# Five units of 128 channels, two k columns a step, and a token mix with tokens on the partitions

## The chip, the cores and the metric

The kernel runs on one core of a Trainium2 chip. The metric is the device time of one execution in microseconds (us). Medians have their lowest and highest value beside them. The engines are TensorE (PE, its weight loads PEld), VectorE (DVE), ScalarE (ACT), GpSimd (POOL) and SyncE (SP), which issues most DMAs.

## The reference, cut to what matters

```python
# x: 2048 tokens x 640 channels, bf16; F = 1728, Fh = 864
h = layernorm(q) * (1 + ca) + sa                  # sa..gb: six rows of silu(c) @ w_mod
k_shift = short_conv(k, shift_k)                  # four taps
kv = k_shift * v
y  = irfft(rfft(pad(kv)) * rfft(pad(ssm_k)))[:S]  # long convolution over the tokens
y  = y + kv * ssm_D
x  = q + ga * (h * y)
h  = layernorm(x) * (1 + cb) + sb
z  = gelu(h @ w_in)                               # 640 -> 1728
z2 = layernorm(z[..., 864:])
g  = w_sp @ z2 + b_sp                             # token mix: 2048 x 2048
x  = x + gb * ((z[..., :864] * g) @ w_out)
```

I name its parts by time: the **start** (tables, short convolution, first transforms), the **mixer** (the long convolution by matrix products: stage 1, a forward product `pu`, a frequency product `T` on VectorE, an inverse product `pz`), the **hole** (TensorE has little to do while the last unit goes through residual, layer norm and transposes), the **gated part** (the projection to `z`) and the **back end** (token mix and output projection).

## The kernel before

Channels go through the mixer in units of 128, 192, 192 and 128. Every instruction of the front part is put into a plan with a planned cost and a priority; a list scheduler fixes each engine's order at build time.

```python
UNITS = ((0, 128), (128, 192), (320, 192), (512, 128))
SLOTS = dict(X=3, X1=3, KH=17, T=4, Z=2, ZT=2, wm=1, big=2, dg=2, st1=2, s1=2, pu=3, pz=2, py=1)
# ...
# stage 1: two channel groups per PSUM tile, two such tiles, emptied by ScalarE
ps = new(name, "s1", [P, 2, NJ * 8], F32)
for i in range(2):
    mm(ps[:, i, :], tl[X][:, cp + i, :], F1flat, True, True)
# ... e.copy(dst, ps)
# one k column of one unit
pu = new(name, "pu", [P, 2, DUM], F32)
mm(pu[:, :, 0:du], M2[:, 0, kc, :], x[:, 2 * kc:2 * kc + 2, 0:du], True, False)
mm(pu[:, 0, 0:du], M2[:, 2, kc, :], xi, False, False)
mm(pu[:, 1, 0:du], M2[:, 1, kc, :], xr, False, True)
# ... product: T_ = pu x KH, [P, 2, 2, du], on VectorE; then six matmuls of the inverse product
# residual and statistics of a unit: one statistic per unit and token tile
op({"DVE": 120 + 0.85 * du}, lambda e, n=n: e.bn_stats(out=st2[:, n, u, :], in_=xt[:, n, d0:d0 + du]), ...)
# ...
# back end: channels on the output partitions (seven channel tiles, the last one short)
for tci in range(S // TC):
    for ft in range(NFT):
        ps = psB.tile([P, TC], F32, tag="mm", bufs=6, name="ps")
        for st_i in range(NT):
            nc.tensor.matmul(ps[:fsz[ft], :], lhsT=tl["hz%d" % (st_i // TB)][:, zo:zo + fsz[ft]],
                             rhs=wT[:, st_i, tci * TC:(tci + 1) * TC], start=(st_i == 0), stop=(st_i == NT - 1))
        # VectorE: add the bias, multiply by z1T[ft]
for n in range(NT):
    ...  # output projection of token tile n, all 16 after the whole mix
```

## Time and profile before

| kernel before, profiled execution | us from the span's start |
|---|---|
| first inverse product | 39.03 |
| end of the last inverse product | 147.6 |
| first matmul of the gated part | 166.93 |
| first matmul of the token mix | 231.21 |
| span | 362.2 |

The median is 364.14 us (363.43 to 364.27, 3 executions). The page's rows, the table by stage, the three forms and VectorE's hole are shown in the prediction below. A row of slices has one digit for each fortieth of the span, the busy share in tenths. In a list in order of time the first number is the start, the second the length of a run of like instructions, and a bracket at the end says how long the engine idled before them and what it waited for.

What such a list shows as a matmul's length has a modelled end. The true price is read from starts: a group of six forward matmuls starts 0.44 us before what follows it, although its length is given as 0.60. The prices read so in the kernel before (median ns from one matmul's start to the next) are 25 for one column, 29 for 64, 56 for 128, 82 for 192, 109 for 256, 136 for 320, 162 for 384, 183 for 432 and 216 for 512; at them its 2374 matmuls come to 310.9 us. I therefore also sum the streaming price of all matmuls between two instants, as the prediction does, and compare it with the elapsed time.

The mixer's waits of TensorE as the profile lists them, in the kernel before (total, times, longest):

```profile
PE s L269 <- ACT X L430: 1.6, 7, 0.3
PE s L269 <- DMA wm<-in_w_mod_dram: 0.5, 1, 0.5
PE pz L269 <- DVE T L465: 0.3, 2, 0.2
PE py L269 <- DMA ZT<-Z: 0.2, 1, 0.2
```

That is 2.6 us. The mixer streams 100.5 us in 108.5, so 8 us are lost. The list shows less because it counts a wait from the modelled end of the matmul before it, 0.16 us after the next could have started, and leaves out what is then under 0.15 us. For instance, the rows of the list in order of time have four stage-1 fills of 256 columns from 67.67 and the next from 68.72: 1.05 us for 0.44 us of streaming, with one bracket of 0.18. Counted from start to start, the waits over 0.06 us in the kernel before are 30 and cost 7.8 us: 15 of them, 4.6 us, are for ScalarE's stage-1 copies, and eight, 1.4 us, for `T`. Between the others TensorE goes from one tile's matmuls to another's without loss.

### The profile page before, as it was taken

To read this page: it belongs to the slowest core of one execution; us is meant where nothing else is said; L and a number is where in the kernel's file an instruction comes from. 1 tells how busy PE (TensorE), PEld (TensorE's weight loads), DVE (VectorE), ACT (ScalarE), POOL (GpSimd) and SP (SyncE) were. 2 spreads that over 40 slices of the span, in tenths; PEclk is the share of its full clock that TensorE was granted. 3 is DMA by queue.
4 is the path that set the end of the run, shared out by engine and by line. 5 is a ranking of instruction groups with operands and counts; after the bars stand their busy time and mean duration, and the time that the engine had idled before them with its cause. 6 is when DMAs were issued, how large, how long until landed. Compare 5 with 4: busy or idle time off the path is not lost.

```text
span 362.2 us, 6081 instructions
## 1 busy us (share of the span) xinstructions
PE 328.2 (91%) x2374; PEld 201.8 (56%) x2374; DVE 223.0 (62%) x492; ACT 153.3 (42%) x324; POOL 117.1 (32%) x133
## 2 busy tenths in 40 slices
PE   1777999899999999709999999999999999999996
PEld 0225787567778888504545654444444444446774
DVE  6769999673749889999893883024233232334553
ACT  6359878967797865605557555300000000000000
POOL 7773611159208999661131011740000000000000
PEclk9989999999999999966999999999999999999999
DMA  7889959869889379100009999510000000000221
GB/s 123 186 242 235 194 201 225 157 91 251 175 223 212 114 157 179 48 1 2 0 9 224 219 205 243 153 31 0 14 2 0 14 2 0 0 2 36 93 91 72
DMA packets 110084, 40.08 MB, mean 111 GB/s; under 512 B 95368, under 2 KB 109288, under 8 KB 110056
## 3 DMA queue, kind: packets, MB, share of 16 engines
q1 hardware_dynamic: 108560, 39.18, 49.4%
q0 software_dynamic: 192, 0.52, 0.7%
q8 instruction: 18, 0.29, 0.3%
q10 hardware_dynamic: 1304, 0.00, 0.2%
q14 instruction: 10, 0.08, 0.1%
HBM read 16.63 MB, written 5.24 MB: 60 GB/s over the span
## 4 chain that ended last, share of the span: by engine, by line
PE 82%; DVE 7%; ACT 6%; POOL 2%; DMA 1%; issue 1%; POOLq 0%; DVEq 0%; ACTq 0%
PE ps L863 27%; PE pu L269 19%; PE pz L269 16%; PE s L269 9%; PE ps L875 8%; ACT X L430 4%; DVE st L698 1%; PE s L787 1%; DMA ZT<-Z 1%; POOL T L366 1%; PE py L269 1%; DVE gh L652 1%; PE pu L680 1%; POOL T L365 1%; DVE T L465 0%
## 5 line engine op out<-in xcount | busy, mean ns | idle before, releaser
L863 PE MATMUL ps<-wT,X 128*128 128x512 bf16 (+1 forms) x336 | 77.1, 379 | 0.0
L866 DVE TENSOR_TENSOR gt<-ps,bsp 128x512 bf16<-128x512 f32 (+1 forms) x28 | 19.3, 691 | 75.2 <-PE ps L863 54.6
L465 DVE TENSOR_TENSOR T<-pu,KH 128x512 bf16<-128x512 f32 (+1 forms) x64 | 50.7, 819 | 14.9 <-PE pu L269 12.3
L863 PEld LDWEIGHTS <-X 128*128 128x128 bf16 (+1 forms) x336 | 34.1, 101 | 38.4
L269 PE MATMUL pu<-X,M 128*128 128x128 bf16 (+3 forms) x384 | 48.6, 254 | 1.1 <-ACT KH L453 1.1
L430 ACT CAST X<-s 128x512 bf16<-128x512 f32 x80 | 44.0, 592 | 8.0 <-PE s L269 7.2
L269 PE MATMUL pz<-T,G 128*128 128x192 bf16 (+3 forms) x384 | 45.2, 255 | 0.3 <-DVE T L465 0.3
L269 PEld LDWEIGHTS <-X 128*128 128x128 bf16 x280 | 26.4, 100 | 21.8 <-issue 10.4
L269 PEld LDWEIGHTS <-M 128*128 128x128 bf16 x384 | 33.0, 98 | 8.9 <-issue 1.4
L269 PEld LDWEIGHTS <-G 128*128 128x128 bf16 x384 | 32.2, 98 | 6.8 <-DVE T L465 0.8
L269 PE MATMUL s<-F1bd,X 128*128 128x256 bf16 x160 | 29.5, 276 | 5.5 <-DVE big L526 2.3
L482 ACT CAST Z<-pz 128x256 bf16<-128x256 f32 (+1 forms) x64 | 27.2, 430 | 14.2 <-PE pz L269 12.7
L269 PE MATMUL s<-big,dg 128*128 128x512 bf16 x80 | 23.5, 441 | 10.6 <-DMA big<-in_A_k_dram 8.0
L863 PE MATMUL ps<-wT,Z 128*128 128x512 bf16 (+1 forms) x112 | 28.7, 379 | 0.0
L453 ACT CAST KH<-pu 128x256 bf16<-128x256 f32 (+1 forms) x64 | 25.3, 432 | 5.3 <-PE pu L269 4.4
L629 POOL TENSOR_TENSOR gh<-gh,gca_bf 128x512 bf16<-128x512 bf16 (+1 forms) x16 | 22.2, 1400 | 11.2 <-DVE gca_bf L595 11.2
L877 DVE TENSOR_TENSOR ot<-ps,xt 128x320 bf16<-128x320 f32 x32 | 15.7, 491 | 14.2 <-PE ps L875 14.2
L695 POOL TENSOR_TENSOR xt<-xt,gh 128x768 bf16<-128x768 bf16 (+1 forms) x12 | 17.7, 1506 | 20.1 <-DVE gh L656 20.1
L875 PE MATMUL ps<-w_o,G 128*128 128x320 bf16 (+1 forms) x128 | 22.7, 299 | 0.0
L269 PEld LDWEIGHTS <-big 128*128 128x128 bf16 (+1 forms) x140 | 14.1, 102 | 15.2
L629 POOL TENSOR_TENSOR gh<-gh,gsa_bf 128x512 bf16<-128x512 bf16 (+1 forms) x16 | 22.2, 1399 | 0.8
L269 PEld LDWEIGHTS <-dg 128*128 128x128 bf16 x80 | 8.5, 108 | 21.6 <-issue 8.8
(138 smaller groups left out, 447.9 us busy)
## 6 DMA issues: line engine op xcount, KB each, us to landing
wm<-in_w_mod_dram SPq DMA_DIRECT2D x8, 400.0 KB, 3.9
kv_scr<-big SPq DMA_DIRECT2D x5, 512.0 KB, 3.3
xt<-in_A_q_dram SPq DMA_DIRECT2D x2, 1280.0 KB, 6.4
out_dram<-ot SPq DMA_DIRECT2D x16, 160.0 KB, 1.8
big<-in_B_w_in_dram SPq DMA_DIRECT2D x2, 1080.0 KB, 7.0
X<-in_A_ssm_k_dram SPq DMA_DIRECT2D x2, 768.0 KB, 9.6
X<-kv_scr SPq DMA_DIRECT2D x2, 768.0 KB, 6.6
wm<-in_w_mod_dram SPq DMA_DIRECT2D x4, 320.0 KB, 3.3
```

Source lines behind the costliest of these rows:

```text
L269: nc.tensor.matmul(o, lhsT=w, rhs=x, start=start, stop=stop)
L365: e.tensor_scalar(tl[v][:], tl[v][:], pidx[:, 0:1], 1.0 / 8192.0, op0=ALU.mult, op1=ALU.mult)
L430: e.copy(dst, tl[name][:].rearrange("p i (j g) -> p i j g", g=8))
L453: op({"ACT": act_cost(2 * du)}, lambda e: e.copy(tl[KH][:, :, 0:du], tl[pk][:, :, 0:du]), r=[pk], w=[KH], t=t)
L465: e.tensor_tensor(T_[:, :, :, 0:du], tl[pu][:, :, None, 0:du].to_broadcast([P, 2, 2, du]), tl[KH][:, None, :, 0:du].to_broadcast([P, 2, 2, ...
L482: op({"ACT": act_cost(2 * du)}, lambda e: e.copy(tl[Z][:, 0:du // 4, 2 * kc:2 * kc + 2, :], tl[pz][:, :, 0:du] .rearrange("p r (q c) -> p ...
L629: lambda e, vec=vec, o=o: e.tensor_tensor(gvu, gvu, vec[:, None, d0:d0 + du].to_broadcast([P, TB, du]), op=o),
L695: op(eng, lambda e: e.tensor_tensor(sl, sl, gh[:, g * TB:(g + 1) * TB, d0:d0 + du], op=ALU.add), r=[("gh", (u, g))], w=[("xt", (u, n)) for ...
L863: nc.tensor.matmul(ps[:fsz[ft], :], lhsT=tl["hz%d" % (st_i // TB)][:, zo:zo + fsz[ft]], rhs=wT[:, st_i, tci * TC:(tci + 1) * TC], start=(s ...
L866: nc.vector.tensor_tensor(gt[:fsz[ft], :], ps[:fsz[ft], :], bsp_bc[:fsz[ft], :], op=ALU.add)
L875: nc.tensor.matmul(ps[:, :HS], lhsT=z1T[ft][:fsz[ft], n * P:(n + 1) * P], rhs=w_o[:fsz[ft], ft, h * HS:(h + 1) * HS], start=(ft == 0), sto ...
L877: nc.vector.tensor_tensor(ot[:, h * HS:(h + 1) * HS], ps[:, :HS], xt[:, n, h * HS:(h + 1) * HS], op=ALU.add)
```

## The change

The intent is to make the units equal (five of 128 channels), so that a step can take two k columns in one PSUM tile (fewer, wider instructions on VectorE and ScalarE), to give one statistic to two units, and to turn the back end round: tokens on the output partitions leave no short channel tile, the bias becomes a column, product and bias are one VectorE instruction, and each token tile is projected soon after its mix. The product then has channels in the free dimension and must be turned; a DMA transpose does it, and TensorE for the last tile. The first half of the gated projection is turned likewise. The priorities of the plan are new.

```diff
-UNITS = ((0, 128), (128, 192), (320, 192), (512, 128))
+NU = 5
+DU = 128
+KP = 2
+S1C = 4
-SLOTS = dict(X=3, X1=3, KH=17, T=4, Z=2, ZT=2, wm=1, big=2, dg=2, st1=2, s1=2, pu=3, pz=2, py=1)
+SLOTS = dict(X=4, X1=4, KH=9, T=4, Z=3, ZT=1, ZTp=2, wm=1, big=2, dg=2, st1=2, s1=1, sm=2, pu=2, pz=2)
...  (new priorities WANT; SECOND says how much later a second choice of engine may be)
@@ stage 1: four channel groups per PSUM tile, one such tile
-                    ps = new(name, "s1", [P, 2, NJ * 8], F32)
-                    for i in range(2):
+                    ps = new(name, "s1", [P, S1C, NJ * 8], F32)
+                    for i in range(S1C):
                         mm(ps[:, i, :], tl[X][:, cp + i, :], F1flat, True, True)
@@ forward product: two k columns
+                pu = new(name, "pu", [P, KP, 2, DU], F32)
+                for k in range(KP):
+                    kc = st * KP + k
+                    mm(pu[:, k], M2[:, 0, kc, :], x[:, 2 * kc:2 * kc + 2, :], True, False)
+                    mm(pu[:, k, 0], M2[:, 2, kc, :], x[:, 2 * kc + 1, :], False, False)
+                    mm(pu[:, k, 1], M2[:, 1, kc, :], x[:, 2 * kc, :], False, True)
@@ frequency product: one instruction of 1024
+                T_ = new(T, "T", [P, KP, 2, 2, DU])
+                e.tensor_tensor(T_[:], tl[pu][:, :, :, None, :].to_broadcast([P, KP, 2, 2, DU]),
+                                tl[KH][:, :, None, :, :].to_broadcast([P, KP, 2, 2, DU]), op=ALU.mult)
@@ statistics: units 0 and 1 together, 2 and 3 together, 4 alone
+            if u not in (1, 3, 4):
+                return
+            us = range(u - (u < 4), u + 1)
...  (gated part: z1 with tokens on the partitions)
@@ back end
+    def mix(t):
+        u = us[t % UB]
+        for fc in range(NFC):
+            ps = psB.tile([P, 512], F32, tag="mm", bufs=4, name="ps")
+            for s_ in range(NT):
+                nc.tensor.matmul(ps[:, :FC], lhsT=wTs[t][:, s_, :], rhs=tl["z2_%d" % (s_ // TB)][...],
+                                 start=(s_ == 0), stop=(s_ == NT - 1))
+            nc.vector.scalar_tensor_tensor(u[:, sl], ps[:, :FC], bcol[:, t:t + 1], z1[t][:, sl], op0=ALU.add, op1=ALU.mult)
+        if t < NT - 1:
+            nc.sync.dma_start_transpose(uTs[t][:], u[:])
+            return
+        ...  (last tile: seven TensorE transposes and one copy)
+    for t in range(NT + 2):
+        if t < NT:
+            mix(t)
+        if t + WB - 1 < NT:
+            load_w(t + WB - 1)
+        if t >= 2:
+            project(t - 2)
```

## The prediction

> **What bounds the kernel now.** I read the page first, then the groups by form, then a table by stage, then the lists in order of time of TensorE and of VectorE around the two places where TensorE waits.
>
> The page's busy shares and its row of slices:
>
> ```profile
> PE 328.2 (91%) x2374; PEld 201.8 (56%) x2374; DVE 223.0 (62%) x492; ACT 153.3 (42%) x324; POOL 117.1 (32%) x133
> ...
> PE   1777999899999999709999999999999999999996
> DVE  6769999673749889999893883024233232334553
> ```
>
> TensorE (PE) is full from slice 5 to the end (a slice is 9.06 us), except the first 40 us and one hole at slices 17 and 18, around 150 to 165 us, where VectorE (DVE) is at 9. The stages, cut where the lists show the work change:
>
> ```profile
> 8.00:39.00 31.00, 23.54 (x138) 12.16 (x138) 25.61 (x67) 20.98 (x49) 19.53 (x29) 0.94 0.98 212
> 39.00:148.00 109.00, 105.40 (x1110) 82.93 (x1108) 84.66 (x153) 82.03 (x194) 60.90 (x55) 1.00 0.83 182
> 148.00:167.00 19.00, 7.59 (x98) 5.91 (x99) 18.70 (x55) 6.60 (x10) 9.65 (x7) 0.72 0.00 1
> 167.00:231.40 64.40, 64.40 (x363) 33.67 (x361) 42.05 (x109) 37.98 (x66) 11.88 (x16) 0.98 0.72 148
> ```
>
> Columns after the stretch and its length: busy time of PE, PEld, DVE, ACT, POOL (instructions), granted clock, DMA share, GB/s. The sequence mixer (39 to 148 us) is PE's, and so are the gated part (167 to 231) and everything after it. Start and hole belong to chains of other engines. Three forms set what PE's time is worth:
>
> ```profile
> L863 PE MATMUL ps<-wT,X 128*128 128x512 bf16 x288 | 66.1, 379 | 0.0
> L430 ACT CAST X<-s 128x512 bf16<-128x512 f32 x80 | 44.0, 592 | 8.0 <-PE s L269 7.2
> L465 DVE TENSOR_TENSOR T<-pu,KH 128x768 bf16<-128x768 f32 x32 | 29.7, 953 | 12.2 <-PE pu L269 11.0 <-ACT Z L482 0.7 <-PE pz L269 0.4
> L465 DVE TENSOR_TENSOR T<-pu,KH 128x512 bf16<-128x512 f32 x32 | 21.0, 685 | 2.7 <-PE pu L269 1.3 <-ACT KH L453 0.5 <-issue 0.3
> ```
>
> 379 ns is one matmul's modelled duration, not its price: the chain of waits has the token mix as one piece,
>
> ```profile
> 231.38 96.69 PE ps L863 x448
> 328.07 30.57 PE ps L875 x224
> ```
>
> so 512 columns cost 96.69/448 = 215.8 ns and 320 columns 30.57/224 = 136.5 ns.
>
> [...] 215.8 and 136.5 ns, and 182.7 ns for 432 columns (5 in 0.9135 us in the gated part). I price matmuls so. [...] in the hole the granted clock is 0.72 and the first five 432-column matmuls take 1.8 us. [...] The two T rows give (953-685)/256 = 1.05 ns an element, about 149 ns fixed, so 1024 elements should take 1.22 us. [...] The change gives each step more columns but fewer buffers, which is my main doubt.
>
> **The change, part by part.** All numbers of instructions are from the two programs' order lists.
>
> *PE work.* [...] all of before is 310.9 us in 2374 matmuls, of after 307.5 in 2657. So the span of 362 holds 51 us that is not PE streaming, and the change removes only 3.4 us of streaming:
> - Token mix: 448 matmuls of 512 become 512 of 432 (tokens on the output partitions, so no short seventh channel tile): 96.7 to 512 x 182.7 ns = 93.5, -3.2 us.
> - First half of the gated projection, turned likewise: 140 of 512 (30.2 us) to 160 of 432 (29.2), -1.0 us.
> - Units of 128 instead of 192: the same columns, 192 more matmuls in the mixer, +0.5 us; seven small transposes for the last tile, +0.4.
>
> *The back end.* Each of 16 tiles has 5.85 us of mix and 1.91 us of projection, issued two tiles late. Its product goes out by a DMA transpose on the queue that also brings the next weight tile. Before, the 16 weight transposes took SyncE 1.7 to 3.0 us each to issue and landed after 4.3 to 6.2; with the product's smaller one and a store I estimate 5 us of queue per 7.76 us tile, and the result is wanted about 12 us later, so nothing waits. VectorE falls from two instructions (691 and 425 ns) to one of 432 from PSUM (0.60 us by the fit): idle there anyway, worth nothing. The last tile's product must pass VectorE and PE's transposes while PE waits: about 0.9 us of wait, in +1.3 with the transposes. Mix, projection and end: 124.1 + 1.3 + the 3.5 us that before has after its last matmul = 128.9, against 130.8: **-1.9 us**.
>
> *The gated part.* 61.75 us of streaming against 62.8, plus the 1.65 us that before loses to the cold clock: 63.4 against 64.45, **-1.0 us**.
>
> *The mixer.* Per pair of k columns VectorE's product is one instruction of 1024: 40 x 1.22 = 48.9 against 50.7 us. ScalarE's stage-1 copies go from 80 x 592 ns to 40 of 1024 (0.85 ns an element by the KH rows, about 1.03 us): 41 against 47 us. Both lie beside PE. What counts is what PE had done when the first inverse product (pz) started: before 15.6 us of streaming at 39.03, after 20.6, because more taps and forward products stand ahead of it. But VectorE also has five more tap products (5 x 0.62), one more layer norm statistic (1.07), four normalisations (4 x 0.42) and one copy less (0.65) ahead of its first T: 5.2 us, of which I let half go into its idle time there (some 7 us before its first T at 37.86): 39.0 + 2.5 = 41.5 us for the first pz (estimate). From there before ran 100.5 us of streaming in 108.6, 93%. After has 96.4 left; with fewer handovers I take 95%: 101.5 us, last pz at 143.0 instead of 147.6: **-4.6 us**.
>
> *The hole.* Before, from the last pz to the first gated matmul at 166.93 is 19.3 us: VectorE's chain of multiplications, statistics and normalisation:
>
> ```profile
> 152.02 1.63 DVE L652 TENSOR_TENSOR gh<-gh,wm 128x512 bf16<-128x512 bf16 x1
> 154.18 1.65 DVE L698 BATCH_NORM_STATS2 st<-xt 128x6 f32<-128x192 bf16 x6
> 162.66 1.45 DVE L778 TENSOR_SCALAR Z<-xt,mv,rstd 128x640 bf16<-128x640 bf16 x4
> ```
>
> After has fewer statistics (48 instead of 64, two units in one; 404 ns for 256 elements by the rows of 342 ns for 192 and 280 for 128: 17.4 against 19.9 us), of which perhaps 1.5 us fall here. Against it: all four multiplications of unit 3 stand behind the last T (4 x 0.68 against 2, +1.4), and the modulation ahead of the first gated matmul is five on ScalarE alone (5 x 0.775 = 3.9 us) where before shared it with VectorE (3 and 2): +1.5. Minus 0.4 for small things: 20.3, **+1.0 us**.
>
> Sum: -4.6 + 1.0 - 1.0 - 1.9 = -6.5 us; 364.14 - 6.5 = **357.6, I say 357.5 us**, 1.8% less.
>
> **The rivals.**
> - *The new buffers bind the mixer.* Stage 1 has one PSUM buffer, filled in 0.43 us and emptied in 1.03 plus two handovers, and pu has two buffers instead of three: about 3.1 us of fill and empty per step over two, 1.55 us against 2.4 us of PE per step. For it: before, ScalarE's stage-1 copies already led the chain for 3 to 4 us near 67 and 104 us. Against it: PE has other work in between, and 1.55 is below 2.4. At 90% instead of 95% the mixer takes 5.6 us longer: 363 us.
> - *The schedule is better than I credit.* Its priorities are new, and residual additions and modulation may go to VectorE. If the start costs no more than before (39 us) and PE runs at 97%, the last pz is at 138.4, and a hole without the +1.0 gives 352 us.
> - *The DMA transposes of the product wait behind weights and stores.* If each tile cost 1 us of wait: 373 us. Against it: 5 us of queue in 7.76 and two tiles of slack. I give it 5%.
>
> **Range and chances.** The start is uncertain by 2 us, the mixer by 4, the hole by 2, the back end by 1.5: together about 5. I take 351 to 364. Two per cent faster is 356.9, just under my figure: faster 0.42, same 0.53, slower 0.05.
>
> **What would show it.** Token mix plus projection as one stretch of 125 to 126 us with PE at 9 throughout; 432-column matmuls at 182.7 ns apart; no wait of PE on uT above 0.5 us; T about 1.22 us; first pz at 40 to 43 us, last at 140 to 146; the first gated matmul 19 to 22 us after that, with VectorE full. I am wrong if PE's row drops below 9 in the mixer with ScalarE's stage-1 copy or pu as the releaser, if PE waits on uT or wT after 230 us, or if the hole shrinks by over 3 us.

The sums of streaming (310.9 us before, 307.5 after) are estimates; the prices, read from starts, also give 310.9 for the kernel before. The 1.65 us of the gated part is 64.45 us elapsed less 62.8 of streaming: its first ten 432-column matmuls take 3.34 us, at a granted clock of 0.50 to 0.59, and ten later ones 1.83.

## The result and the profile after

The changed kernel takes **359.32 us** (median of 4, 358.34 to 360.74), the kernel before 363.88 in the same rounds (363.43 to 364.27). The ratio is 0.9878, with a 95% interval of 0.984 to 0.9916: 1.2% less time, "same" at a threshold of 2%. A ratio here and below is the mean time of one kernel's fast executions over the mean of the kernel before's in the same rounds on the same chip, so it isn't quite the ratio of the medians.

TensorE is busy for 322.1 us (90%) and VectorE for 220.4 (62%) in the changed kernel. Their rows of slices on its page:

```profile
PE   1757999989999999808999999999999999999996
...
DVE  6788974999799989699865646722232333232233
```

TensorE's row (counted from 0, a slice is 8.95 us) has an 8 in the mixer at slice 8, 72 to 81 us. VectorE's row is at 9 there, but the one listed wait in that slice is of a stage-1 fill for ScalarE's copy, 1.1 us: the prediction's own sign of being wrong in the mixer has come once. The row has the hole at slices 16 to 18, and 9 from there to the end. The stages, in the same columns as the table in the prediction:

```profile
44.30:148.00 103.70, 99.28 (x1253) 86.97 (x1257) 88.03 (x129) 69.14 (x106) 57.68 (x54) 1.00 0.73 179
148.00:165.40 17.40, 7.09 (x101) 5.57 (x102) 14.66 (x46) 7.68 (x11) 6.04 (x6) 0.72 0.03 2
165.40:229.10 63.70, 63.70 (x383) 35.24 (x381) 42.95 (x95) 44.70 (x81) 15.02 (x19) 0.97 0.26 59
229.10:354.50 125.40, 124.69 (x744) 72.16 (x742) 37.90 (x68) 1.44 (x2) 3.89 (x3) 1.00 0.45 94
```

The mixer starts 5.3 us later than before and ends at the same time; the hole is shorter; so is the back end. Against the prediction, in the two profiled executions:

| step | before | after | moved | predicted |
|---|---|---|---|---|
| first inverse product at | 39.03 | 44.32 | +5.3 | +2.5 |
| last inverse product ends at | 147.6 | 147.6 | 0.0 | -4.6 |
| hole (to the first gated matmul) | 19.36 | 17.73 | -1.6 | +1.0 |
| gated part (to the first token-mix matmul) | 64.29 | 63.72 | -0.6 | -1.0 |
| back end (to the end of the span) | 130.97 | 128.81 | -2.2 | -1.9 |
| span | 362.2 | 357.9 | -4.3 | -6.5 |

The three forms that carried the argument, from the page of the changed kernel (groups: busy us, mean ns, idle before and releaser):

```profile
L872 PE MATMUL ps<-X,wT 128*128 128x432 bf16 x512 | 95.7, 346 | 0.0
...
L477 DVE TENSOR_TENSOR T<-pu,KH 128x1024 bf16<-128x1024 f32 x40 | 48.0, 1215 | 5.7 <-PE pu L276 4.2
...
L298 ACT CAST X<-s 128x1024 bf16<-128x1024 f32 x40 | 40.8, 1019 | 15.5 <-PE s L276 15.4
```

1215 and 1019 ns are the estimated 1.22 and 1.03 us. The token mix has no idle time ahead of it, and it costs what was estimated: six groups of 16 take

```profile
229.07 17.68 PE L872 MATMUL ps<-X,wT 128*128 128x432 bf16 x96
246.59 2.07 PE L890 MATMUL po<-w_o,uT 128*128 128x320 bf16 x14
```

17.52 us from the first start to the next, 182.5 ns each. So the sizes of single instructions were right. What the mixer waits for is new. TensorE's waits between 44 and 148 us, changed kernel:

```profile
PE pz L276 <- DVE T L477: 1.8, 5, 0.5
PE pu L276 <- DVE T L477: 1.1, 2, 0.6
PE s L276 <- ACT X L298: 1.1, 1, 1.1
```

4.0 us of listed waits instead of 2.6, and 2.9 of them are for the frequency product: the inverse product waits for `T` itself, and a forward product for a `pu` buffer that `T` still reads. The mixer streams 96.4 us in 103.3, so 6.9 us are lost. Counted from start to start as above:

| TensorE's waits in the mixer, us | before | after | after, repeat (experiment 1) |
|---|---|---|---|
| for ScalarE's stage-1 copies | 4.6 | 1.8 | 1.8 |
| for `T` | 1.4 | 4.0 | 3.0 |
| all | 7.8 | 6.6 | 5.4 |

(Six matmul records are missing from the trace of the first profile; the gaps that they leave aren't counted.)

So the wider steps took 2.9 us of stage-1 waits away, as intended, and gave 1.6 to 2.5 us of that back in waits for `T`.

### The profile page after: what moved, and what is told of

Same layout as the page of the kernel before. It is cut to its first block, busy times and chain, and to the rows that moved or that the text cites. A ratio compares the mean times of both kernels' runs of the same rounds, so it can differ in the third digit from the quotient of the medians.

```text
span 357.9 us, 6480 instructions
## 1 busy us (share of the span) xinstructions
PE 322.1 (90%) x2651; PEld 215.9 (60%) x2657; DVE 220.4 (62%) x434; ACT 149.2 (42%) x239; POOL 109.7 (31%) x130
## 4 chain that ended last, share of the span: by engine, by line
PE 73%; DVE 15%; ACT 4%; DMA 2%; issue 2%; POOL 2%; DVEq 0%; POOLq 0%; ACTq 0%
PE ps L872 26%; PE pz L276 15%; PE pu L276 15%; PE po L890 9%; PE sm L276 4%; DVE T L477 4%; PE s L276 3%; DMA ZT<-Z 2%; ACT X L298 2%; DVE st L564 2%; DVE st L707 1%; DVE gh L587 1%; PE sm L791 1%; DVE big L541 1%; ACT KH L298 1%
## 5 line engine op out<-in xcount | busy, mean ns | idle before, releaser
L872 PE MATMUL ps<-X,wT 128*128 128x432 bf16 x512 | 95.7, 346 | 0.0
L872 PEld LDWEIGHTS <-wT 128*128 128x128 bf16 x512 | 50.1, 98 | 42.2
L477 DVE TENSOR_TENSOR T<-pu,KH 128x1024 bf16<-128x1024 f32 x40 | 48.0, 1215 | 5.7 <-PE pu L276 4.2
L276 PE MATMUL pu<-X,M 128*128 128x128 bf16 (+1 forms) x480 | 46.5, 241 | 2.4 <-DVE T L477 1.1
L276 PEld LDWEIGHTS <-Z 128*128 128x128 bf16 x320 | 31.5, 100 | 26.8 <-issue 2.1
L298 ACT CAST X<-s 128x1024 bf16<-128x1024 f32 x40 | 40.8, 1019 | 15.5 <-PE s L276 15.4
L276 PE MATMUL pz<-T,G 128*128 128x128 bf16 (+1 forms) x480 | 41.9, 237 | 1.8 <-DVE T L477 1.8
L276 PE MATMUL pu<-big,Z 128*128 128x432 bf16 x160 | 35.6, 354 | 0.0
L276 PE MATMUL pz<-big,Z 128*128 128x432 bf16 x160 | 35.4, 353 | 0.0
L890 PE MATMUL po<-w_o,uT 128*128 128x320 bf16 (+1 forms) x224 | 32.8, 299 | 0.0
L298 ACT CAST Z<-pz 128x512 bf16<-128x512 f32 x36 | 21.2, 589 | 17.6 <-PE pz L276 17.5
```

Of the source, the lines that this page charges most:

```text
L276: nc.tensor.matmul(o, lhsT=w, rhs=x, start=start, stop=stop)
L298: (e.copy if e is nc.scalar else e.tensor_copy)(dst, src)
L477: e.tensor_tensor(T_[:], tl[pu][:, :, :, None, :].to_broadcast([P, KP, 2, 2, DU]), tl[KH][:, :, None, :, :].to_broadcast([P, KP, 2, 2, DU] ...
L872: nc.tensor.matmul(ps[:, :FC], lhsT=wTs[t][:, s_, :], rhs=tl["z2_%d" % (s_ // TB)][:, s_ % TB, fc * FC:(fc + 1) * FC], start=(s_ == 0), st ...
L890: nc.tensor.matmul(ps[:, :HS], lhsT=uTs[t][:fsz[ft], ft, :], rhs=w_o[:fsz[ft], ft, h * HS:(h + 1) * HS], start=(ft == 0), stop=(ft == NFT ...
```

## The experiments

Profiled executions of one and the same front differ: its first inverse product lay between 43.5 and 46.6 us in the profiles that leave the start's work as it is. One cause can be read in the lists. The second group of eight tap matmuls, in the repeat of the changed kernel (experiment 1) and in experiment 11, whose start is the same:

```profile
12.46 1.89 PE L276 MATMUL sm<-big,dg 128*128 128x512 bf16 x8 [0.94 <-DVE big L541]
```

```profile
12.47 3.57 PE L276 MATMUL sm<-big,dg 128*128 128x512 bf16 x8 [1.00 <-DVE big L541]
```

It runs at full or at half rate from one execution to the next. Why, isn't shown: the profile's granted clock is 1.00 from 7 to 14 us both in the changed kernel, where four of these matmuls have begun by 14 us, and in experiment 6, where all eight have. So times are compared by their ratios, and single profiles only for lengths that repeat: the hole of this front was 17.7 us in all nine profiles of kernels that keep its work (the clock experiment, with extra matmuls in it, had 17.6).

Kernels 1 to 4 shared one chip, 5 to 8 a second, 9 to 11 a third, 12 a fourth.

### 1 to 3: which half gave the time?

**1** is the changed kernel again, on the chip of 2 to 4. **2** has the changed front and the earlier gated orientation and back end; **3** has the earlier front with the changed `z1` orientation and back end. The front's instruction order is that of the kernel it is taken from.

```diff
 # 2: front of the changed kernel
-    z1 = [... one tile per 128 tokens ...];  for t in range(NT + 2): mix(t) ... project(t - 2)
+    z1T = [... one tile per 128 channels ...];  for tci ...: for ft ...  (as before);  for n ...: project
 # 3: front of the kernel before
-    z1T = [...];  for tci in range(S // TC): ...
+    z1 = [...];  for t in range(NT + 2): mix(t); load_w(t + WB - 1); project(t - 2)
```

> The changed kernel once more, as the base of this series. 0.988 of before (359.3 to 359.7 us), the first pz near 44.3 us, the last pz ending near 147.5, the first gated matmul near 165.4 and the first matmul of the token mix near 229.

> The changed kernel's front (five units, two k columns per step, its schedule) with the gated projection and the back end of before; the order of instructions up to the gated part is that of the changed kernel. Theory: the mixer gained nothing (last pz at 147.5 in both traces) and the hole gave 1.6 us, so this is 1.6 us faster than before, about 362.3 us, ratio 0.995 to 0.997. Rival (the mixer's saving is real and the back end gives it back [...]): 358 to 360 us, ratio below 0.99.

> Before's front with the changed gated projection (tokens on partitions) and the changed back end. Theory: 2.0 us from token mix, projection and end and 0.7 to 1.0 us from the gated part, about 361.2 us, ratio 0.991 to 0.993. Rival (the back end gives nothing): ratio 1.0 within 0.2%.

| kernel | median us (range) | ratio to before (95%) |
|---|---|---|
| 1 changed kernel again | 358.48 (356.74 to 360.40) | 0.9881 (0.9848 to 0.9914) |
| 2 front only | 361.63 (359.78 to 364.27) | 0.9986 (0.9942 to 1.0029) |
| 3 back end and `z1` only | 360.42 (358.79 to 360.86) | 0.9933 (0.9908 to 0.9958) |

Experiment 1 has the expected ratio; its profile's four marks (43.5, 145.5, 163.3 and 226.2 us) come 0.8 to 2.8 us earlier than expected. The interval of experiment 2 holds the theory's 0.995 to 0.997 and excludes the rival's 0.99; that of experiment 3 holds the theory's figure and excludes the rival's. The back end and the turned `z1` give 0.7% (2.4 us; the profile has its token mix at 230.0 and its span at 358.8, so 128.8 us again). The front gives 0.1%, within its interval of nothing: about 0.5 us with 1.6 either way, where the prediction summed -3.6 us (-4.6 and +1.0). By profiles its first gated matmul comes at 165.2 us (mean of 165.3, 163.3, 164.7 and, in experiment 9 with the same front, 167.6) against 166.5 (166.9 and 166.1), 1.3 us sooner. The parts sum to 0.8% where the whole has 1.2%; the intervals cover that, so no interaction is claimed.

### 4: take VectorE's first layer norm away (a miss)

```diff
-            op(LN1, stats, r=xs, ...)
+            op({"POOL": 120}, lambda e: e.memset(mv1[:, n, :], 0.01), r=xs, ...)   # wrong on purpose
```

> Wrong result on purpose: the 16 layer norm statistics (16 x 1.07 us on VectorE) are replaced by a small GpSimd memset of the mean and variance; all else stays. Theory (VectorE, full from 60 to 85 us and busy with eight statistics in a row from 27 to 33 us, holds PE back in the mixer): the last pz ends 4 to 8 us earlier, the time is 352 to 356 us. Rival (the buffers of stage 1 and of pu hold PE, not VectorE): less than 2 us faster, the last pz at 146 or later.

Measured: 367.93 us (366.3 to 368.48), ratio 1.0139 (1.0114 to 1.0165), so slower than both kernels with 17 us of VectorE less. Both expectations fell, and the reason lies in the experiment itself: with another planned cost and engine for 16 instructions the scheduler made another order of everything. TensorE's waits in its mixer, where the changed kernel has 4.0 us:

```profile
PE s L276 <- ACT X L298: 4.0, 4, 1.1
PE pu L276 <- DVE T L477: 3.6, 3, 1.9
...
```

From 109 to 123 us TensorE was busy for 8.46 of 14 us. The priorities belong to one set of costs. From here on every experiment keeps the planned costs, and so the order, and changes only what an instruction does.

### 5 to 8: what holds the mixer and the start?

Theory V is VectorE; its rival S is the single stage-1 PSUM tile, which ScalarE must empty before TensorE may fill it again. All keep the changed kernel's order; 5, 6 and 7 compute a wrong result (it stayed within the tolerance), 8 is right.

```diff
 # 5: no first layer norm statistics on VectorE
-    e.bn_stats(...) twice; e.bn_aggr(out=mv1[:, n, :], in_=st[:])
+    e.memset(mv1[:, n, :], 0.01)
 # 6: T for one of the two k columns, read twice
-    e.tensor_tensor(T_[:], tl[pu][:, :, :, None, :]..., tl[KH][:, :, None, :, :]..., op=ALU.mult)
+    e.tensor_tensor(T_[:, 0:1], tl[pu][:, 0:1, :, None, :]..., tl[KH][:, 0:1, None, :, :]..., op=ALU.mult)
 # 7: half of each stage-1 copy, read twice by the forward product
-    copy(e, dst, tl[name][:]...)
+    copy(e, dst, tl[name][:, 0:S1C // 2]...)
 # 8: two stage-1 PSUM tiles of half the size, two copies of 512
-    ps = new(name, "s1", [P, S1C, NJ * 8], F32)
+    tl[name] = [psA.tile([P, S1C // 2, NJ * 8], F32, tag="s1" + h, bufs=1, name="s1" + h) for h in "ab"]
```

> The changed kernel with the order of all instructions kept as it is (the planned costs are untouched), but the 16 first layer norm statistics (two statistics and one aggregate each, about 1.07 us of VectorE per tile, 17 us in all) replaced by one tiny memset of VectorE; wrong result on purpose. This mends the fault of the earlier run, whose order changed. Between its first inverse product (44.3 us) and its last (147.6) the changed kernel streams 96.4 us on TensorE in 103.3, so a mixer that waits for nothing can gain 6.9 us there, plus what the start gains. Theory V, VectorE holds the mixer and the start: first inverse product 2 to 5 us earlier (8 statistics stand before the first T), last one's end 5 to 9 us earlier, kernel 1.5 to 2.5% faster than the changed kernel, about 350 us. Rival S, the single stage-1 PSUM buffer and its handovers to ScalarE hold it: last inverse product less than 2 us earlier, kernel within 0.6% of the changed one, about 357 us.

> The changed kernel, order kept, with the frequency product T computed for one of its two k columns only (512 elements instead of 1024, about 0.68 instead of 1.22 us, 21 us of VectorE less in all) and read twice by the inverse product; TensorE's matmuls are the same in number and size; wrong result on purpose. It cuts VectorE's load and the latency of a step. Theory V (VectorE holds the mixer): last inverse product ends 5 to 8 us earlier, kernel 1.3 to 2.2% faster than the changed one; the first one moves by under 1 us, since T comes last in the start. Rival S (stage 1): less than 2 us earlier.

> The changed kernel, order kept, with each of the 40 stage-1 copies of ScalarE cut to half its elements (512 instead of 1024, about 0.6 instead of 1.02 us), the forward product reading the copied half twice; TensorE's matmuls are the same in number and size; wrong result on purpose. The one stage-1 PSUM buffer is then emptied 0.42 us sooner, 17 us of ScalarE in all. Rival S (the single stage-1 buffer holds the mixer): last inverse product ends 4 to 7 us earlier, of which 1.7 us (four copies of the first unit) in the start. Theory V (VectorE holds the mixer): the start gains 1 to 2 us, and the stretch from first to last inverse product stays within 1.5 us of 103.3.

> The changed kernel, order kept and result right, with the stage-1 PSUM buffer of four channel groups split into two of two groups each, and each copy of ScalarE into two of 512 elements (about 0.6 us each, 1.2 us instead of 1.02 together). The copy can start after two matmuls instead of four, and the next two matmuls after the first copy: TensorE and ScalarE overlap at the handover, at the price of 0.18 us of ScalarE per copy (7 us in all). Rival S: last inverse product 2 to 4 us earlier, kernel 0.5 to 1.1% faster than the changed one. Theory V: within 1.5 us of the changed kernel, in either direction, in the stretch from first to last inverse product; start 0.5 to 1 us earlier at most.

| kernel | median us (range) | ratio to before (95%) | first `pz` | from first to last `pz` |
|---|---|---|---|---|
| changed, two profiles | see above | 0.9881 (0.9848 to 0.9914) | 44.3, 43.5 | 103.3, 102.1 |
| 5 no statistics | 357.75 (355.63 to 358.88) | 0.9854 (0.9821 to 0.9888) | 45.1 | 101.2 |
| 6 half of T | 355.58 (354.97 to 356.11) | 0.9798 (0.9774 to 0.9822) | 42.5 | 100.3 |
| 7 half of each copy | 355.68 (355.23 to 356.94) | 0.9809 (0.9783 to 0.9835) | 43.5 | 101.8 |
| 8 stage 1 split | 357.64 (355.60 to 358.43) | 0.9845 (0.9815 to 0.9876) | 44.4 | 101.9 |

No single cause holds the mixer. Halving T gives 0.8% (3 us), less than the 1.3 to 2.2% that theory V wanted; halving the copies gives 0.7% where S wanted more. Taking 17 us of other work off VectorE gives 0.3%, not resolved from nothing; in its mixer the waits for `T`, counted from starts, fall to 1.7 us. It leaves the first inverse product where it was (45.1 us) although eight statistics, 8.6 us of VectorE, went from ahead of it. TensorE's pace doesn't hide a gain: in experiments 9 and 11 it was as slow there as in 5 (the second to fourth stage-1 fills are listed at 1.01 us each in all three, at 0.60 in the changed kernel's first profile), and all three take 23.5 us from the first stage-1 fill to the first inverse product. VectorE merely idles longer in experiment 5:

```profile
37.17 0.69 DVE L406 COPY G<-sm 128x1024 bf16<-128x1024 bf16 x1 [9.73 <-PE sm L404]
```

**VectorE's statistics aren't what the start waits for.** Its other work there was not taken away, and part of it is on the chain of waits (see why the prediction was right). In experiment 6 the waits for T are gone from the list, from 44 us to the end of its mixer:

```profile
PE s L276 <- ACT X L298: 1.1, 1, 1.1
PE sm L276 <- DMA ZT<-Z: 0.6, 1, 0.6
PE pu L276 <- ACT X L298: 0.2, 1, 0.2
```

and its mixer still takes 100.3 us for 96.4 us of streaming. So 2 to 3 us of the mixer belong to T. Of the 3.6 us that TensorE still waits there, counted from starts, 2.4 are for stage-1 copies and 0.8 for one DMA transpose. Where the 2.6 us of experiment 7 lie, its one profile doesn't tell: its mixer is 0.3 to 1.5 us shorter (its stage-1 waits fall to 0.8 us and those for `T` rise to 4.1, counted from starts) and its start within the spread. Splitting the stage-1 tile shortens its one listed wait to 0.5 us but isn't told apart from the changed kernel by its time.

### 9: TensorE instead of the DMA turns the product

```diff
-        if t < NT - 1:
-            nc.sync.dma_start_transpose(uTs[t][:], u[:])
-            return
+    def turn(t):          # called after mix(t + 1), for every tile
         pt = psB.tile([P, NFT, P], BF16, tag="pt", bufs=1, name="pt")
```

> The changed kernel with the product of each tile turned by seven TensorE transposes (issued after the next tile's mix) instead of by a DMA transpose; result right, front unchanged. The changed kernel already turns its last tile so. Theory (the DMA transposes are wholly hidden, so that turning by DMA saves just the TensorE time of the alternative): 15 tiles x 7 transposes of 128 columns x 55.8 ns = 5.9 us more in the stretch from the first token-mix matmul to the last matmul, 131.3 instead of 125.4 us, kernel about 1.6% slower than the changed one. Rival (the DMA turning costs waits or slows the weight transposes on the same queue): less than 4 us more. If the transposes bring waits for VectorE's product or for the copies out of PSUM: more than 8 us.

Measured: 363.12 us (361.96 to 366.41), ratio 1.0009 (0.9977 to 1.0041). Against the changed kernel's 0.9881 that is 1.3%, 4.6 us; from the first token-mix to the last matmul the profile has 130.4 us instead of 125.4.

```profile
242.28 0.56 PE L882 MATMUL pt<-ident,u 128*128 128x128 bf16 x7
242.67 6.00 PE L872 MATMUL ps<-X,wT 128*128 128x432 bf16 x32
```

Seven transposes take 0.39 us from start to start, 15 times 5.85 us, and the stretch grew by 5.0. Most of what is short comes back at the end, where the changed kernel waits 0.65 us for its last product and this one doesn't. So the DMA transposes are hidden completely, and **with TensorE's transposes in their place the change gains nothing that these runs resolve**: its whole gain is about the TensorE time that they save.

### 10: T in two halves

```diff
-                e.tensor_tensor(T_[:], ...)                      # 1024 elements
+                for k in range(KP):
+                    e.tensor_tensor(T_[:, k:k + 1], ...)         # 512 elements each
```

> The changed kernel, order kept and result right, with each frequency product T of 1024 elements written by two VectorE instructions of 512, one for each k column, so that the inverse product's first half can start after the first. It costs VectorE a fixed 0.15 us 40 times, 6 us more (88 of the mixer's 103 us are busy there now), and brings the first half 0.53 us sooner. The earlier runs left open whether the waits for T come from VectorE's load or from the latency of one wide instruction: taking 17 us of other work off VectorE moved the mixer by 1 to 2 us, halving T by 2 to 3 us. Latency theory: the mixer (first to last inverse product) 0.5 to 2 us shorter than 102 to 103, kernel 0.2 to 0.6% faster. Load theory: mixer 1 to 3 us longer, kernel 0.3 to 0.9% slower.

Measured: 360.48 us (359.07 to 361.4), ratio 0.9930 (0.9906 to 0.9955), 0.5% slower than the changed kernel by the two ratios, though their intervals touch (0.9906 to 0.9914). TensorE's waits between 44 and 148 us:

```profile
PE pu L276 <- DVE T L478: 1.8, 4, 0.9
...
PE pz L276 <- DVE T L478: 0.2, 1, 0.2
```

The inverse product's listed wait shrank from 1.8 to 0.2 us, but that doesn't show the latency theory's gain: counted from starts it waits 1.1 us, in seven short waits that the list leaves out, as much as in experiment 1 (1.15) and 0.9 less than in the first profile of the changed kernel (2.1). The wait for a free `pu` buffer rose from 1.9 to 2.8 by the same count (1.1 to 1.8 listed), as VectorE needs 2 x 678 ns for a step instead of 1215. The mixer takes 103.8 us, 0.5 and 1.7 us longer than the two profiles of the changed kernel (103.3 and 102.1), near the lower edge of the load theory's 1 to 3. So the sign is the load theory's, as far as the intervals tell.

### 11: fewer statistics in the hole

```diff
-   lambda e, n=n: e.bn_stats(out=st2[:, n, ...], in_=xt[:, n, ...])
+   lambda e, n=n: e.memset(st2[:, n, ...], 0.5) if u > 1 else e.bn_stats(...)   # wrong on purpose
```

> The changed kernel, order kept, with the 32 second layer norm statistics of units 2 and 3 (256 elements, 0.37 us) and of unit 4 (128 elements, 0.23 us) replaced by tiny memsets of VectorE; wrong result on purpose. Of them 13 lie between the last T and the first normalisation of the gated part, 4.1 us there. Theory H (the hole is VectorE's chain, and how many statistics are left at the end of the mixer sets its length: the kernel before has 30 of them there, 7.9 us): the hole of 17.7 us from the last inverse product to the first gated matmul shrinks by 2.5 to 3.5 us, kernel 0.7 to 1.1% faster than the changed one. Rival (the last unit's transposes, ScalarE's copies and GpSimd's residual additions set the hole, VectorE waits for them anyway): hole shorter by less than 1.2 us.

(The list has 14 statistics there, not 13.) Measured: 356.33 us (354.68 to 357.65), ratio 0.9818 (0.9794 to 0.9843), 0.6% below the changed kernel; the hole is 15.4 us, 2.3 less. Compare VectorE in the hole of the changed kernel,

```profile
146.42 0.68 DVE L666 TENSOR_TENSOR gh<-gh,sm 128x512 bf16<-128x512 bf16 x1
147.89 0.69 DVE L666 TENSOR_TENSOR gh<-gh,sm 128x512 bf16<-128x512 bf16 x1 [0.79 <-PE sm L276]
...
151.75 0.42 DVE L662 TENSOR_TENSOR gh<-gh,wm 128x512 bf16<-128x512 bf16 x1
...
153.22 1.41 DVE L707 BATCH_NORM_STATS2 st<-xt 128x6 f32<-128x256 bf16 x4 [0.45 <-POOL xt L701]
...
160.81 1.50 DVE L782 TENSOR_SCALAR Z<-xt,mv,rstd 128x640 bf16<-128x640 bf16 x4
```

with that of experiment 11:

```profile
154.74 0.84 DVE L662 TENSOR_TENSOR gh<-gh,wm 128x512 bf16<-128x512 bf16 x1 [0.91 <-ACT wm L660]
...
159.49 1.51 DVE L782 TENSOR_SCALAR Z<-xt,mv,rstd 128x640 bf16<-128x640 bf16 x4 [0.60 <-POOL rstd L224]
```

The statistics are on the hole's path (4.1 us of them gone, 2.3 us won), just short of what theory H expected and well over its rival. The rest went into two waits that then showed: 0.91 us for ScalarE's copy and 0.60 for GpSimd's reciprocal root.

### 12: keep TensorE's clock up

Experiment 8, plus matmuls that nobody reads: 70 before the first data, four behind each stage-1 fill of the first unit, 48 in the hole.

```diff
+        def keep_warm(n, x, cols=256, tag="s1a"):
+            for i in range(n):
+                mm(out_[:, 0:cols], ident[:], x, True, True)     # result never read
```

> The changed kernel with its stage-1 buffer split as in the run of that name (357.6 us there, 0.9845 of the kernel before), plus matmuls whose results nobody reads, to keep TensorE's clock up: 70 of 128 columns before the first data arrive, four of 256 columns after each stage-1 fill of the first unit, and 48 of 256 columns in the hole. Result right, order of all other instructions unchanged. Reason: in the start the second group of eight 512-column tap matmuls takes 3.57 us in some executions of the same front and 1.89 us in others, and the first group always 3.57; in the hole the granted clock is 0.50 from 156 to 168 us, eight transposes take 1.79 us there instead of about 0.6, and five 432-column matmuls 2.01 us instead of 0.91. Theory C (a cold clock costs time in start and hole): first tap group about 1.9 us, first inverse product at 41 to 43 us instead of 42.5 to 46.5, hole 0.4 to 0.9 us shorter (16.8 to 17.3), gated part 62.2 to 62.7 us instead of 63.0 to 64.0, kernel 0.6 to 1.3% faster than with the split buffer alone, 353 to 355.5 us. Rival D (other engines set the start and the hole, so that a faster TensorE there only waits longer): gated part about 1 us shorter, start and hole within 0.5 us, kernel within 0.4% of 357.6 us.

Measured: 356.76 us (355.95 to 357.62), ratio 0.9825 (0.9800 to 0.9850), 0.2% below experiment 8, so by time the rival's figure. By stage it is mixed. The start gained: both tap groups run at full rate (1.89 us each), and the first inverse product comes at 42.0 us instead of 44.4 (one profile each). The first group's own gain is lost again: the second starts at 12.45 us as ever, after a wait of 2.26 us for VectorE. The hole stayed at 17.6 us, although the granted clock (the third number from the end) was 1.00 until 160 us. Windows of this kernel, in the late hole and at the start of the gated part:

```profile
157.50:159.00 1.50, 1.09 (x8) 0.62 (x9) 1.47 (x5) 0.13 (x1) 0.00 (x0) 1.00 0.01 5
...
160.00:161.40 1.40, 0.83 (x10) 0.62 (x8) 1.33 (x7) 1.40 (x3) 0.00 (x0) 0.86 0.09 0
161.40:163.20 1.80, 1.80 (x8) 0.78 (x6) 1.70 (x8) 1.78 (x3) 0.86 (x2) 0.50 0.86 74
```

The hole is therefore not set by TensorE's clock. The granted clock fell to 0.50 at about 161 us all the same, after 1.5 us of idling and three short waits, so the gated part (64.0 us) gained nothing, and what a full clock is worth there stays open. This kernel computes the right result and is the fastest right one: 1.7% below the kernel before, and by the two ratios 0.6% below the changed one, with intervals that just overlap (0.9848 to 0.9850).

## Why the prediction was right

The total was right (357.5 predicted, 359.32 measured, inside 351 to 364, and "within 2%" as the likeliest class), but two of its four terms were wrong, by +4.6 and -2.6 us, and partly cancelled. That these errors have opposite signs is luck. By its own steps:

- **Back end, -1.9: right.** -2.2 in the profile by the mix's first start, with 182.5 ns for a 432-column matmul and no wait on the DMA's product (SyncE's queue was held for 1.22 + 2.45 + 0.53 us for one tile's product, weight and store, 4.2 where I had estimated 5). Experiment 3 confirms it alone (with `z1`, -2.4 us by time), experiment 9 that the turning is hidden. Two small sizes: VectorE's product took 668 ns, not 600; the last tile's wait was 0.65 us, not 0.9.
- **Gated part, -1.0: right in sign, -0.6 measured.** The slow first matmuls stand in both kernels: the first ten of 432 columns take 3.34 us before and 3.60 after, at a granted clock of 0.50 to 0.59 and of 0.50, instead of 1.83.
- **Mixer, -4.6: wrong, 0.0 measured.** Two steps failed: 2.8 us lie in the start (44.3 instead of 41.5) and 1.8 in the mixer (103.3 instead of 101.5). First, "5.2 us, of which I let half go into its idle time there" priced the start by VectorE's extra work. Experiment 5 took 8.6 us of statistics from there, and its first inverse product was no earlier. The figure beside it was the better guide: TensorE has 5.0 us more to stream before the first inverse product, and that product came 5.3 us later (4.4 to 8.4 over all profiles of the two starts). All of the 5.0 us lie after the first forward product (11.4 us of streaming instead of 6.4), and from there to the first inverse product the kernel before takes 10.1 us (10.4 in experiment 3), the changed front 14.6 to 15.4 in five profiles, and 14.5 in experiment 12, where the granted clock was 1.00. The chain of waits runs through other engines as well. In the kernel before, that stretch has 6.6 us of ScalarE on it and nothing of VectorE; after, it has 4.2 us of VectorE, in the last 7 us before the first inverse product (start, length, what):

```profile
37.80 1.64 DVE gh L587 x2
39.45 0.60 DVE big L541
...
40.09 1.90 PE sm L276 x8
...
43.06 1.22 DVE T L477
```

  So two of the normalisations and two of the tap products that the prediction counted are on the path, and the statistics aren't. How much of the 5.3 us is TensorE's added streaming and how much this VectorE work, no run isolated. With the extra matmuls of experiment 12 in the start, the first inverse product came some 2 us earlier (42.0 instead of 44.4 us in experiment 8, one profile each). Second, "with fewer handovers I take 95%": it was 93.3% (94.4% in the repeat). The waits for stage-1 copies fell by 2.9 us, but those for `T` and its buffers rose by 2.5 (1.6 in the repeat), as the first rival feared. The rival named stage 1 and `pu` buffers; both do show, but the waits and experiment 6 put `T` first.
- **Hole, +1.0: wrong, -1.6 measured.** Its terms, from VectorE's lists between the last T and the first gated normalisation (sums of listed lengths):

| on VectorE in the hole | before | after | predicted to move |
|---|---|---|---|
| statistics | 30, 7.85 us | 14, 4.08 us | -1.5 |
| multiplications by the mixer's result in PSUM | 4, 2.71 us | 6, 4.09 us | +1.4 |
| multiplications by ScalarE's copies of it, residual | 4, 4.41 us | 4, 2.34 us | (not priced) |
| idle | 0 | 3.12 us | (not priced) |

  The statistics were mis-sized: not only do two units share one, more of them also found room before the last T, so -3.8 us. The +1.4 held. Fewer bf16 instructions ran behind GpSimd's additions (a product of 512 took 1.63 and 1.28 us before; after, 1.14, and 0.42 where it started ahead of them), and VectorE now idles for TensorE's and ScalarE's last turns. From the last T to the first normalisation it took 14.3 us instead of 15.8, where these terms and the 0.4 for small things made -0.5. The modulation was priced at +1.5 and cost 0.3: from the first normalisation to the first gated matmul 4.5 us instead of 4.3. ScalarE works at its five tiles from 162.69 to 166.37, but the first gated matmul, which needs only the first of them, starts at 165.35.

## What to carry to other kernels

Price a changed start by the engine whose work grew on the path, and ask of each other engine whether taking its work away would move anything. Here fewer, wider steps took stage-1 waits away (4.6 to 1.8 us) but left fewer buffers, and the waits moved to the wide instruction in the middle (1.4 to 4.0 us, 3.0 in the repeat); count both, and count waits from start to start, since a list can leave short ones out. When an order comes from a scheduler, test with edits that keep its costs, or the experiment measures another order.

## What these traces show of TensorE's prices, its clock and GpSimd

- Each matmul here has its own weight load: 448 matmuls of 512 columns took 215.8 ns each (kernel before), and seven of 128 columns 55.7 ns each (experiment 9, 0.39 us from start to start).
- In experiment 12 the granted clock fell to 0.50 at about 161 us. The longest gap of TensorE after 154 us had been 1.5 us, and it was busy for 0.03 of 1.5, 1.09 of 1.5, 0.36 of 1.0 and 0.83 of 1.4 us before it; all 20 matmuls of that stretch were transposes. In the kernel before, the last matmul ended at 155.76 and the granted clock was 0.59 from 156 to 158 us. What makes it fall, no run here shows.
- A bf16 product or sum of 128x512 on VectorE took 0.36 to 0.43 us where no GpSimd instruction ran beside it. In the kernel before, the product that started 1.35 us before the end of one of GpSimd's additions took 1.63 us, and that which started 1.00 us before the end of another took 1.28: each the rest of the addition and 0.28 us. What holds it up, no run here isolates.
